# Hedgehog attention beside a Mish layer: the sum of phi(k) times v, two heads crossed in 64 columns or four heads apart in 32

## The chip, the cores and the metric

One core of one Trainium2 chip runs the whole program. The time is the device time of one execution in microseconds (us). The kernel before was run three times: 153.95, 154.15 and 154.91 us, so the median is 154.15 us. A separate execution was recorded by the profiler; the rows shown come from it. Engines are named as in the profile: PE (TensorE matmul; PEld are its weight loads), DVE (VectorE), ACT (ScalarE), POOL (GpSimd), SP (SyncE, which issues most of the transfers).

## The reference: what is computed

```python
def _A_ref(x, wqkv, w_phi, wo):                 # S = 2048, D = 448, H = 16 heads, Dh = 28
    q, k, v = ...                               # x @ wqkv, split into heads
    pq = jnp.einsum("bhsd,hdf->bhsf", q, w_phi)
    pk = jnp.einsum("bhsd,hdf->bhsf", k, w_phi)
    phi_q = jnp.concatenate([_softmax(pq, axis=-1), _softmax(-pq, axis=-1)], axis=-1)
    phi_k = jnp.concatenate([_softmax(pk, axis=-1), _softmax(-pk, axis=-1)], axis=-1)
    kv = jnp.einsum("bhsf,bhsd->bhfd", phi_k, v)
    z  = jnp.einsum("bhsf->bhf", phi_k)
    num = jnp.einsum("bhqf,bhfd->bhqd", phi_q, kv)
    den = jnp.einsum("bhqf,bhf->bhq", phi_q, z)[..., None] + 1e-6
    return (num / den, heads put side by side) @ wo

def _B_ref(x, w1, b1, w2):                      # F = 1792
    h = x @ w1 + b1
    return (h * tanh(softplus(h))) @ w2         # Mish

xn = _layernorm(x)
return x + _A_ref(xn, ...) + _B_ref(xn, ...)
```

The change concerns `kv` and `z`: for each head a sum over all 2048 tokens of phi(k), 28 positive and 28 negative features, times v (28 columns) and times ones.

## The kernel before, in words

The 2048 tokens are 16 tiles (t) of 128, taken in eight pairs (u). Layer norm runs on DVE, ACT and POOL, and the normalized pairs are transposed, by PE at the start and by DMA later. From them PE makes v (`v_mm`), the exponents of k (`k_mm`) and of q (`q_mm`), and the hidden layer of the Mish branch in 28 pieces (`ffn1`, f0.n and f1.n, each in two parts of 8 and 6 matmuls; all these matmuls are issued at line 438). Each takes a pair of PSUM banks out of four pairs; the planner's `take2` gives the pair used least recently, and `free2` gives it back.

ACT writes exp(+-k) into `E_of(u)`. `k_norm` (steps kn u.s) sums it per head on DVE (L631), inverts the sums (L633), and POOL multiplies the product phi(k) in place (L635). ACT also makes the exponentials of q (L684) and Mish (L703); it loads another table between the two.

`v_all` holds, for each token and head, the 28 columns of v and two columns of ones, so that the same matmul gives `kv` and `z`. `kv_mm` (steps kv2 kv3 kv5 kv1 kv4 kv6 kv0 kv7, line 652) adds a pair of tokens tiles to one PSUM bank: the stationary operand is 60 columns of `v_all`, two neighbouring heads, and the moving one the 2 x 56 features of the same two heads. Its results stand in two groups of rows, 0 to 59 and 64 to 123 (r = 0, 1). A result thus holds four blocks: two of a head with itself, and two of one head with the other, which are not wanted. `kvz` (L664, two operations on DVE) adds the epsilon of the denominator (`epsT`, made in `eps_rows`), multiplies by `mask2`, which is 1 on the wanted blocks and 0 on the crossed ones, and writes `KVT` as bf16. Then one DMA transpose (kvT, L670, queue of SP) turns `KVT` into `KVZ`.

The steps nd0 to nd15 (line 726) multiply the transposed phi(q) (`EqT`, DMA transposes at L692, steps e0 to e15) with `KVZ`: for each tile 16 matmuls of 56 rows and 60 moving columns. DVE makes numerator over denominator from the result (L741 to L752). Then come the output projection, the second matmul of the Mish branch (L866, L828, L844), the sum with x on DVE (L793) and the stores.

POOL begins with constants: `mask` (pm), `Wbd` (pw), the zero columns of phi(q) (pp), `mask2` and zeros in `KVT` (pk, L350 to L359), the identity `ident` (pi), later the ones in `v_all` (pv). The identity is used by PE's transposes, the first of which are at L561.

The order of all steps is written out by hand in `ORDER`; each engine does its share of the steps in that order. Waits are put in by the program from what each step reads and writes. Behind the sums the order is: kv7, f1.13 part 1, f1.7 part 1, f0.5 part 1, kvz, f0.8 part 1, and then the second parts; nd3 is the first nd, and e15, e1 and e0 stand behind kvT in SP's queue.

Of the kernel before, what the change touches and what calls it, by code (L numbers as in the profile page):

```python
# [30 lines left out]
def ap_on(src, dims):  # L31
    return bass.AP(tensor=src.tensor, offset=src.offset, ap=[list(src.ap[0])] + [list(d) for d in dims])
# [112 lines left out]


ORDER = """
pm pw lx3s pp pk lx1s lkms lkts st6d lpa table pi st7a st2d st3d rs3t xn3d lvms rs1a z16 xn1d bd wtk0b wtk1b lx2s xt3b
pv xt1d wmk0b wmk1a lqT0 st5a st4d lqT2 rs2a v31a lqT1 lqT3 qd lx6s v11a lx4s v32d wmq1a lx0s k11 xn2p st15d st14d st10d
l1m0s wmq0a st8d rs7p k12 xn7p st1d st9d k31 xt2m q11 l1m1s k32 v12d rs4p st12d xt7m st11d q31 q12 q32 q21 xn4d rs5p  # L150
st13d v21d rs6a q22 xn5d st0d xt4m k21 xt5m v22d v71a k22 v72a rs0p k71 l1m2s k41 kn3.1 e3 k72 k42 xn6d v41a v51a ep e4
k51 xn0p v42a xt6m kn7.0 e2 k52 v52a kn1.1 xt0m kn7.1 kn5.0 v61a lbs q41 v62d kn4.0 k61 q42 e5 e6 l1ts v01d kn2.1 k62
q51 v02d e7 q52 kn1.0 k01 b1 e10 k02 q61 kn3.0 f1.21 e9 q62 e11 f1.22 f1.31 f0.21 e12 e8 f1.51 e13 f1.32 f1.52 kn5.1 los
f0.22 q71 kn2.0 q01 q72 l2s f0.11 f1.01 kn6.1 q02 f1.02 kn6.0 f0.12 kn4.1 kv2 kv3 kv5 kv1 kv4 kn0.0 kn0.1 kv6 kv0 kv7
f1.131 f1.71 f0.51 kvz f0.81 f1.72 f0.52 f0.82 f1.132 f1.81 f0.131 f1.82 nd3 e15 f1.11 e1 e0 f0.132 f1.12 f1.121 nd2
f1.91 f1.122 nd0 f0.101 f1.92 f0.71 f0.102 nd1 f0.72 f1.41 f0.01 ot1m nd6 e14 f1.42 f0.02 f0.91 f0.31 f0.92 ot0m nd7
f0.32 f0.41 wob f1.101 f0.111 f0.42 f0.61 f1.102 f0.112 nd5 f0.62 f1.111 nd4 f0.121 f1.112 f1.61 f0.122 wo01 f1.62 ot3m
ot2m nd11 nd13 G02 wo11 wo32 nd12 G01 nd10 G11 wo22 wo02 ot6m ot5m G31 wo21 nd15 wo31 G21 G32 G12 wo12 sto1 G62 nd14 nd9
G61 wo51 wo61 G51 G22 ot7m G42 sto0 sto3 nd8 ot4m wo52 G41 wo7F g14 wo62 wo7H wo41 G52 stt14 wo42 sto2 g15 sto5 sto4
# [9 lines left out]
def _kernel(es, nc, A_x, A_wqkv, A_w_phi, A_wo, B_w1, B_b1, B_w2, out):  # L169
    def sb(name, shape, dtype):  # L170
        return es.enter_context(nc.sbuf_tensor(name, shape, dtype))
# [5 lines left out]
    mask = sb("mask", [GP, 4], FP32)  # L177
    Wraw = sb("Wraw", [GP, G, DH], BF16)
    Wbd = sb("Wbd", [GP, G, 2, 64], BF16)
    mask2 = sb("mask2", [P, 2, DH], FP32)  # L180
    b1_rows = sb("b1_rows", [FC, P], BF16)
    b1T = sb("b1T", [P, FC], FP32)
    x_all = sb("x_all", [P, NT, D], BF16)
# [43 lines left out]
    def E_of(u):  # L227
        return actT[:, FE + u, 0:4 * D].rearrange("p (s i d) -> p s i d", s=2, i=2)
# [21 lines left out]
    def bank(b, n=1):  # L250
        return PS[:, b * TCW:(b + n) * TCW]
# [89 lines left out]
        op("POOL", lambda e: e.memset(ap_on(v_flat[:, DH:DH + 2].bitcast(mybir.dt.uint32),  # L341
                                            [[(DH + 2) // 2, NU * 2 * H]]), 0x3F80), w=[("v1",)], tag="pv0")

    def p_pads():
        for i in (1, 2, 0):
            op("POOL", lambda e, i=i: e.memset(Eq_of(i).rearrange("p i s (h n) -> p (i s h) n", n=64)[:, :, QP:64], 0.0),
               w=[("Eqp", i)] + ([(n, h) for n in ("WT", "WU") for h in range(2)] if i == 0 else []), tag=f"pp{i}")

    def p_mask2():
        op("POOL", lambda e: e.memset(mask2[:], 1.0), w=[("mask2",)], tag="pk0")  # L350
        for r in range(2):
            lo, hi = HALF[r]
            op("POOL", lambda e, lo=lo, hi=hi: e.affine_select(
                out=mask2[lo:hi], in_=mask2[lo:hi], compare_op=ALU.is_ge, fill=0.0, base=0, channel_multiplier=1,
                pattern=[[-(DH + 2), 2], [0, DH]]), r=[("mask2",)], w=[("mask2",)], tag="pk1")
            op("POOL", lambda e, lo=lo, hi=hi: e.affine_select(
                out=mask2[lo:hi], in_=mask2[lo:hi], compare_op=ALU.is_ge, fill=0.0, base=DH + 1, channel_multiplier=-1,
                pattern=[[DH + 2, 2], [0, DH]]), r=[("mask2",)], w=[("mask2",)], tag="pk2")
        op("POOL", lambda e: e.memset(KVT[:, :, :, :, :].rearrange("p g s x f -> p (g s x f)").bitcast(mybir.dt.uint32),  # L359
                                      0), r=[("mask2",)], w=[("KVT", 0), ("KVT", 1)], tag="pk3")  # L360

    def eps_rows():
        for i in range(2):
            op("DVE", lambda e, i=i: e.tensor_reduce(epsT[:, i:i + 1], ap_on(ident[:, DH + i:DH + i + 1],
                                                                          [[64, 2], [DH + 2, 2]]), AX.XY, ALU.add),
               r=[("ident",)], w=[("epsT", i)], tag=f"ep{i}")
        op("DVE", lambda e: e.scalar_tensor_tensor(epsT[:, 2:3], epsT[:, 0:1], DEN_EPS / 2, epsT[:, 1:2], ALU.mult,
                                                   ALU.add), r=[("epsT", 0), ("epsT", 1)], w=[("epsT", 2)], tag="ep2")
# [149 lines left out]
    def xT(u, eng):  # L518
        i = u % NXN
        if eng == "DMA":  # L520
            dma("SP", lambda e: e.dma_start_transpose(xnT[:, u, :, :], xn[i][:, :]),
                r=[("xn", i, 0, 0), ("xn", i, 1, 0), ("xn", i, 1, 1)] + ([] if u == 1 else [("x", t) for t in (0, NT - 1)]),
                w=[("xnT", u), ("xnU", u)], tag=f"xTm{u}")
            return
        if eng == "both":
            b = take2(False)
            pe(lambda e: transpose7(e, b, xn[i], 3), [("xn", i, 0, 0), ("xn", i, 1, 0), ("xn", i, 1, 1), ("ident",)],
               [pb(b), pb(b + 1)], f"xT{u}")
            evac("ACT", lambda: xnT[:, u, 0:3, :].rearrange("p c n -> p (c n)"), lambda: bank16(b)[:, 0:3 * P], [pb(b)],
                 [("xnT", u)], f"xTe{u}")  # L530
            evac("DVE", lambda: xnT[:, u, 3:7, :].rearrange("p c n -> p (c n)"), lambda: bank16(b + 1)[:, 0:4 * P],
                 [pb(b + 1)], [("xnU", u)], f"xTf{u}")
            return
        b = take1()
        pe(lambda e: transpose7(e, b, xn[i]), [("xn", i, 0, 0), ("xn", i, 1, 0), ("xn", i, 1, 1), ("ident",)], [pb(b)],
           f"xT{u}")
        evac(eng, lambda: xnT[:, u, :, :].rearrange("p c n -> p (c n)"), lambda: bank16(b)[:, 0:7 * P], [pb(b)],
             [("xnT", u), ("xnU", u)], f"xTe{u}")
# [102 lines left out]
    def kv_mm(u):  # L641
        if not kv_seen:
            kv_bank.append(take2())
        kvb = kv_bank[0]
        kv_seen.add(u)
        first, last = len(kv_seen) == 1, len(kv_seen) == NU

        def f(e):
            for par in range(2):
                for g in range(G):  # L650
                    for r in range(2):
                        ins = e.matmul(bank(kvb)[64 * r:64 * r + NDW, g * 2 * QP:(g + 1) * 2 * QP],  # L652
                                       v_all[:, u, par, 8 * r + 2 * g:8 * r + 2 * g + 2, :],
                                       E_of(u)[:, :, par, (4 * r + g) * QP:(4 * r + g + 1) * QP],
                                       start=(first and par == 0 and g == 0), stop=(last and par == 1),
                                       skip_group_check=True)
            return ins
        pe(f, [("E", u, 0), ("E", u, 1), ("v", u), ("v1",)], [pb(kvb)], f"kv{u}")

    def kvz():  # L660
        kvb = kv_bank[0]
        for r in range(2):
            lo, hi = 64 * r, 64 * r + NDW
            op("DVE", lambda e, r=r, lo=lo, hi=hi: e.scalar_tensor_tensor(  # L664
                ap_on(KVT[lo:hi, 0, 0, r, 0:1], [[P, 2 * G], [1, QP]]),
                ap_on(bank(kvb)[lo:hi, 0:1], [[QP, 2 * G], [1, QP]]), epsT[lo:hi, 2:3],
                ap_on(mask2[lo:hi, 0, 0:1], [[0, 2 * G], [1, QP]]), ALU.add, ALU.mult),
               r=[pb(kvb), ("mask2",), ("epsT", 2)], w=[("KVT", r)], tag=f"kvz{r}")
        free2(kvb)
        dma("SP", lambda e: e.dma_start_transpose(KVZ[:, :, :], KVT[:, :, :, :, :].rearrange("p g s x f -> p (g s x f)")),  # L670
            r=[("KVT", 0), ("KVT", 1)], w=[("KVZ",)], tag="kvT")

# [43 lines left out]
    def nd(t):  # L718
        b = take2(False)

        def f(e):
            for s in range(2):
                for g in range(G):
                    for r in range(2):
                        at = (s * G + g) * NDW
                        ins = e.matmul(bank(b + r)[:, at:at + NDW], EqT[64 * r:64 * r + QP, t, s * G + g, :],  # L726
                                       KVZ[64 * r:64 * r + QP, 2 * g + s, 64 * r:64 * r + NDW], start=True, stop=True)
            return ins
        pe(f, [("EqT", t), ("KVZ",)], [pb(b), pb(b + 1)], f"nd{t}")
        i = t % 2  # L730
# [218 lines left out]
    add("b1", bias_T)  # L949
    add("ep", eps_rows)  # L950
    add("qd", double_qT)
    for n, fn in (("pi", p_ident), ("pm", p_mask), ("pw", p_wbd), ("pv", p_ones), ("pk", p_mask2), ("pp", p_pads)):
        add(n, fn)
    for n in (4, 8, 10, 12, 14, 16, 18, 20):
        add(f"z{n}", warm, n)

# [52 lines left out]
```

## Time and profile before

| | |
|---|---|
| median of three runs | 154.15 us (153.95 to 154.91) |
| the profiled execution | 154.01 us |
| its span, first to last instruction | 152.1 us |
| instructions in it | 4002 |
| mean granted clock of PE | 1.000 |
| HBM read and written | 7.02 MB and 1.84 MB |

The profiled execution takes 1.9 us more than its span, for what lies around the first and the last instruction, and it is 0.14 us below the median. A row of the timeline or of the chain begins with the start and the duration in us; a row of a group has the line, the engine, the operation, the result and its sources, the shapes, the count, the busy time in us, the mean of one in ns, and behind the second bar the idle time before it and what ended it. A matmul's own duration covers its way through the array, so many are in flight at once; the pace is read from the time of a run of them.

### The profile page before, as it was taken

Reading aid. Unit: us, or ns where it says so; the run is one execution under the profiler, and the core shown is the slowest. Engines: PE = TensorE matmul, PEld = TensorE weight load, DVE = VectorE, ACT = ScalarE, POOL = GpSimd, SP = SyncE. Lnnn points to the kernel's source line nnn. Section 1 sums busy time; section 2 is a strip of 40 time slices with the busy share of each in tenths; the row PEclk is TensorE's granted clock in tenths of the full one; section 3 lists DMA queues with packets and bytes.
Section 4 is the critical chain, followed back from the end, with each engine's and each line's share of the span. In section 5 each row is a group of like instructions: output and inputs, shape, how many; then the busy total and the mean of one; then the engine's idle time right before and its main releaser. Section 6 shows DMA issues by size and latency. Waiting matters only on the chain.

```text
span 152.1 us, 4002 instructions
## 1 busy us (share of the span) xinstructions
PE 145.4 (96%) x1735; PEld 76.1 (50%) x1735; DVE 102.4 (67%) x224; ACT 74.1 (49%) x96; POOL 41.4 (27%) x59
## 2 busy tenths in 40 slices
PE   7799997999899999999989999999999999999993
PEld 3475543556455584445434445444555555554552
DVE  0997999999999503059998378999373377252452
ACT  3889989796979994776756387100000000000000
POOL 7704743799899970000000000000000000000000
PEclk9999999999999999999999999999999999999999
DMA  5999759989999998840913510803300016003025
GB/s 136 294 136 337 156 166 161 251 158 136 198 190 173 251 271 207 157 89 0 98 37 59 39 26 0 65 2 65 60 0 4 16 49 181 0 4 60 0 100 201
DMA packets 39997, 17.24 MB, mean 113 GB/s; under 512 B 33964, under 2 KB 39212, under 8 KB 39980
## 3 DMA queue, kind: packets, MB, share of 16 engines
q1 hardware_dynamic: 39372, 16.87, 53.5%
q8 instruction: 13, 0.21, 0.6%
q10 hardware_dynamic: 608, 0.12, 0.4%
q14 instruction: 4, 0.03, 0.1%
HBM read 7.02 MB, written 1.84 MB: 58 GB/s over the span
## 4 chain that ended last, share of the span: by engine, by line
PE 69%; DVE 18%; SPq 6%; DMA 3%; ACT 2%; issue 1%
PE PS L438 32%; PE PS L866 28%; DVE stats L467 4%; PE PS L828 3%; SPq L285 3%; DMA x_all<-in_A_x_dram 3%; DVE v_all L745 3%; DVE v_all L747 2%; PE PS L652 2%; PE PS L726 2%; DVE v_all L749 2%; DVE xn L752 2%; DVE v_all L516 1%; DVE mv L468 1%; ACT actT L684 1%
## 5 line engine op out<-in xcount | busy, mean ns | idle before, releaser
L438 PE MATMUL PS<-xnT,W 64*128 64x512 bf16 x392 | 44.9, 376 | 0.9 <-ACT actT L623 0.5
L866 PE MATMUL PS<-W,actT 64*128 64x448 bf16 x392 | 38.7, 349 | 0.0
L703 ACT ACTIVATE actT<-PS,b1T 128x1024 bf16<-128x1024 f32 x28 | 29.8, 1113 | 13.4 <-PE PS L438 13.3
L438 PEld LDWEIGHTS PS<-xnT,W 64*128 64x128 bf16 x392 | 18.9, 94 | 21.7 <-DVE v_all L747 0.9
L866 PEld LDWEIGHTS PS<-W,actT 64*128 64x128 bf16 x392 | 18.8, 94 | 17.2
L635 POOL TENSOR_TENSOR actT<-actT,rSk 128x896 bf16<-128x896 bf16 x16 | 26.6, 1702 | 1.9 <-DVE rSk L633 1.3
L793 DVE TENSOR_TENSOR x_all<-PS,x_all 128x448 bf16<-128x448 f32 (+1 forms) x16 | 9.1, 615 | 15.8 <-PE PS L866 15.1
L631 DVE TENSOR_REDUCE Sk<-actT 128x32 f32<-128x896 bf16 x16 | 16.8, 1047 | 0.2
L741 DVE COPY Sq<-PS 128x16 f32<-128x16 f32 x32 | 4.0, 167 | 17.1 <-PE PS L726 17.0
L623 ACT ACTIVATE actT<-PS 128x896 bf16<-128x896 f32 x16 | 13.7, 923 | 1.0 <-PE PS L438 0.9
L438 PE MATMUL PS<-Wpk,xnT 64*128 64x448 bf16 x112 | 12.9, 350 | 1.0 <-DVE rSk L633 0.8
L438 PE MATMUL PS<-Wkv,xnT 64*128 64x448 bf16 x112 | 12.6, 349 | 0.0
L438 PE MATMUL PS<-Wpq,xnT 64*128 64x448 bf16 x112 | 12.5, 349 | 0.0
L467 DVE BATCH_NORM_STATS2 stats<-x_all 128x6 f32<-128x448 bf16 x14 | 8.5, 607 | 4.3 <-DMA x_all<-in_A_x_dram 4.3
L749 DVE TENSOR_TENSOR v_all<-v_all 128x464 f32<-128x464 f32 x16 | 10.3, 642 | 0.6
L745 DVE TENSOR_TENSOR v_all<-PS,Sq 128x464 f32<-128x464 f32 x16 | 10.3, 641 | 0.5
L752 DVE TENSOR_TENSOR xn<-v_all,rden 128x448 bf16<-128x448 f32 x16 | 10.0, 625 | 0.6
L747 DVE TENSOR_TENSOR v_all<-PS,Sq 128x464 f32<-128x464 f32 x16 | 10.1, 630 | 0.0
L684 ACT ACTIVATE actT<-PS 128x896 bf16<-128x896 f32 x10 | 8.6, 912 | 1.4 <-PE PS L438 1.4
L438 PEld LDWEIGHTS PS<-Wpk,xnT 64*128 64x128 bf16 x112 | 5.5, 94 | 5.8 <-DVE rSk L633 1.2
L438 PEld LDWEIGHTS PS<-Wpq,xnT 64*128 64x128 bf16 x112 | 6.0, 94 | 4.8
L438 PEld LDWEIGHTS PS<-Wkv,xnT 64*128 64x128 bf16 x112 | 5.8, 94 | 4.8 <-issue 0.6
(88 smaller groups left out, 128.8 us busy)
## 6 DMA issues: line engine op xcount, KB each, us to landing
W<-in_B_w_dram SPq DMA_DIRECT2D x1, 1568.0 KB, 7.5
out_dram<-x_all SPq DMA_DIRECT2D x7, 224.0 KB, 2.1
W<-in_B_w_dram SPq DMA_DIRECT2D x3, 448.0 KB, 4.2
x_all<-in_A_x_dram SPq DMA_DIRECT2D x4, 224.0 KB, 3.8
x_all<-in_A_x_dram SPq DMA_DIRECT2D x2, 448.0 KB, 4.2
Wkv<-in_A_wqkv_dram SPq DMA_DIRECT2D x2, 336.0 KB, 4.6
Wo<-in_A_wo_dram SPq DMA_DIRECT2D x2, 336.0 KB, 5.0
W<-in_B_w_dram SPq DMA_DIRECT2D x2, 224.0 KB, 4.8
```

Of the source, the lines that this page charges most:

```text
L438: ins = e.matmul(o, lhs(c, k), rhs(c, k), start=part == "1" and c == 0, stop=part == "2" and c == 2)
L467: op("DVE", lambda e: e.bn_stats(stats[:, t, :], x_all[:, t, :]), r=[("x", t)], w=[("st", t)], tag=f"bn{t}")
L623: op("ACT", lambda e, s=s: e.activation(E_of(u)[:, s, :, :], two(b, D), ACT.Exp, scale=1.0 if s == 0 else -1.0), r=[pb(b), pb(b + 1)], w=[ ...
L631: op("DVE", lambda e: e.tensor_reduce(Sk[u][:, s, :], Eh(), AX.X, ALU.add), r=[("E", u, s)], w=[("Sk", u, s)], tag=f"Sk{u}.{s}")
L635: op("POOL", lambda e: e.tensor_tensor(Eh(), Eh(), ap_on(rSk[u][:, s, 0:1], [[1, 2 * H], [0, DH]]), ALU.mult), r=[("E", u, s), ("rSk", u, ...
L684: op("ACT", lambda e, s=s: e.activation(Eq_of(u)[:, :, s, :].rearrange("p i (h n) -> p i h n", n=64)[:, :, :, 0:QP], two(b, D).rearrange(" ...
L703: op("ACT", lambda e: e.activation(actT[:, fc, q * 1024:(q + 1) * 1024], bank(b, 2), ACT.Mish, bias=b1T[:, fc:fc + 1]), r=[("b1T",), pb(b) ...
L745: op("DVE", lambda e: e.tensor_tensor(tv(t1[i]), num(0), sx(1), ALU.mult), r=[pb(b), pb(b + 1), ("Sq", i, 1)], w=[("t1", i)], tag=f"ta{t}")
L747: op("DVE", lambda e: e.tensor_tensor(tv(t2), num(1), sx(0), ALU.mult), r=[pb(b), pb(b + 1), ("Sq", i, 0)], w=[("t2",)], tag=f"tb{t}")
L749: op("DVE", lambda e: e.tensor_tensor(t1[i], t1[i], t2, ALU.add), r=[("t1", i), ("t2",)], w=[("t1", i)], tag=f"tc{t}")
L752: op("DVE", lambda e: e.tensor_tensor(o_sb[(t // 2) % 2][:, t % 2, :].rearrange("p (h d) -> p h d", d=DH), t1[i][:, :, 0:DH], ap_on(rden[i ...
L866: ins = e.matmul(bank(places[par][0])[:, 0:D], l, r, start=fresh[par], stop=places[par][2] and i >= len(todo) - 2)
```

## The change

`kv_mm` makes the sum for each head apart. Instead of two heads in 60 stationary columns and 112 moving ones there is one head, 30 stationary and 56 moving columns, and four heads stand in four groups of 32 columns of the array; a step has 32 matmuls instead of 16. No crossed blocks arise, so `mask2` and its making on POOL go. `kvz` becomes four additions on DVE, each on 30 rows and on half the columns. The rows of the second head in a group of 64 begin at 32 instead of 30, so `eps_rows` gathers from rows 32 apart, and nd reads `KVZ` as two runs of 30 columns. Zeros in `KVT` now stand for themselves (`KVT0`). The three zero fills `pp` become three steps in the same order; the rest of `ORDER` is the same. A tag is renamed in `xT`.

```diff
-pm pw lx3s pp pk lx1s lkms lkts st6d lpa table pi ...
+pm pw lx3s pp1 pp2 pp0 pk lx1s lkms lkts st6d lpa table pi ...
...
-    mask2 = sb("mask2", [P, 2, DH], FP32)
...
-    def p_mask2():
-        op("POOL", lambda e: e.memset(mask2[:], 1.0), w=[("mask2",)], tag="pk0")
-        for r in range(2):
-            lo, hi = HALF[r]
-            op("POOL", lambda e, lo=lo, hi=hi: e.affine_select(
...
-            op("POOL", lambda e, lo=lo, hi=hi: e.affine_select(
...
+    def p_zero():
         op("POOL", lambda e: e.memset(KVT[:, :, :, :, :].rearrange("p g s x f -> p (g s x f)").bitcast(mybir.dt.uint32),
-                                      0), r=[("mask2",)], w=[("KVT", 0), ("KVT", 1)], tag="pk3")
+                                      0), w=[("KVT0",)], tag="pk3")
...
             op("DVE", lambda e, i=i: e.tensor_reduce(epsT[:, i:i + 1], ap_on(ident[:, DH + i:DH + i + 1],
-                                                                          [[64, 2], [DH + 2, 2]]), AX.XY, ALU.add),
+                                                                          [[32, 4]]), AX.X, ALU.add),
...
             for par in range(2):
                 for g in range(G):
-                    for r in range(2):
-                        ins = e.matmul(bank(kvb)[64 * r:64 * r + NDW, g * 2 * QP:(g + 1) * 2 * QP],
-                                       v_all[:, u, par, 8 * r + 2 * g:8 * r + 2 * g + 2, :],
-                                       E_of(u)[:, :, par, (4 * r + g) * QP:(4 * r + g + 1) * QP],
+                    for j in range(4):
+                        h = 8 * (j // 2) + 2 * g + j % 2
+                        ins = e.matmul(bank(kvb)[32 * j:32 * j + DH + 2, g * QP:(g + 1) * QP],
+                                       v_all[:, u, par, h, :], E_of(u)[:, :, par, h * DH:(h + 1) * DH],
                                        start=(first and par == 0 and g == 0), stop=(last and par == 1),
...
-        for r in range(2):
-            lo, hi = 64 * r, 64 * r + NDW
-            op("DVE", lambda e, r=r, lo=lo, hi=hi: e.scalar_tensor_tensor(
-                ap_on(KVT[lo:hi, 0, 0, r, 0:1], [[P, 2 * G], [1, QP]]),
-                ap_on(bank(kvb)[lo:hi, 0:1], [[QP, 2 * G], [1, QP]]), epsT[lo:hi, 2:3],
-                ap_on(mask2[lo:hi, 0, 0:1], [[0, 2 * G], [1, QP]]), ALU.add, ALU.mult),
-               r=[pb(kvb), ("mask2",), ("epsT", 2)], w=[("KVT", r)], tag=f"kvz{r}")
+        for j in range(4):
+            lo, hi = 32 * j, 32 * j + DH + 2
+            op("DVE", lambda e, j=j, lo=lo, hi=hi: e.tensor_scalar(
+                ap_on(KVT[lo:hi, 0, 0, j // 2, (j % 2) * DH:(j % 2) * DH + 1], [[P, 2 * G], [1, DH]]),
+                ap_on(bank(kvb)[lo:hi, 0:1], [[DH, 2 * G], [1, DH]]), epsT[lo:hi, 2:3], 0.0, op0=ALU.add, op1=ALU.add),
+               r=[pb(kvb), ("KVT0",), ("epsT", 2)], w=[("KVT", j)], tag=f"kvz{j}")
...
-                                       KVZ[64 * r:64 * r + QP, 2 * g + s, 64 * r:64 * r + NDW], start=True, stop=True)
+                                       KVZ[64 * r:64 * r + QP, 2 * g + s, 64 * r:64 * r + 64].rearrange(
+                                           "p (h c) -> p h c", c=32)[:, :, 0:DH + 2], start=True, stop=True)
```

More of the change, by code (lines that the diff above doesn't have):

```diff
@@ L147 @@
 ORDER = """
[L148 to L156, printed above, removed]
+pm pw lx3s pp1 pp2 pp0 pk lx1s lkms lkts st6d lpa table pi st7a st2d st3d rs3t xn3d lvms rs1a z16 xn1d bd wtk0b wtk1b
+lx2s xt3b pv xt1d wmk0b wmk1a lqT0 st5a st4d lqT2 rs2a v31a lqT1 lqT3 qd lx6s v11a lx4s v32d wmq1a lx0s k11 xn2p st15d
+st14d st10d l1m0s wmq0a st8d rs7p k12 xn7p st1d st9d k31 xt2m q11 l1m1s k32 v12d rs4p st12d xt7m st11d q31 q12 q32 q21
+xn4d rs5p st13d v21d rs6a q22 xn5d st0d xt4m k21 xt5m v22d v71a k22 v72a rs0p k71 l1m2s k41 kn3.1 e3 k72 k42 xn6d v41a
+v51a ep e4 k51 xn0p v42a xt6m kn7.0 e2 k52 v52a kn1.1 xt0m kn7.1 kn5.0 v61a lbs q41 v62d kn4.0 k61 q42 e5 e6 l1ts v01d
+kn2.1 k62 q51 v02d e7 q52 kn1.0 k01 b1 e10 k02 q61 kn3.0 f1.21 e9 q62 e11 f1.22 f1.31 f0.21 e12 e8 f1.51 e13 f1.32 f1.52
+kn5.1 los f0.22 q71 kn2.0 q01 q72 l2s f0.11 f1.01 kn6.1 q02 f1.02 kn6.0 f0.12 kn4.1 kv2 kv3 kv5 kv1 kv4 kn0.0 kn0.1 kv6
+kv0 kv7 f1.131 f1.71 f0.51 kvz f0.81 f1.72 f0.52 f0.82 f1.132 f1.81 f0.131 f1.82 nd3 e15 f1.11 e1 e0 f0.132 f1.12 f1.121
+nd2 f1.91 f1.122 nd0 f0.101 f1.92 f0.71 f0.102 nd1 f0.72 f1.41 f0.01 ot1m nd6 e14 f1.42 f0.02 f0.91 f0.31 f0.92 ot0m nd7
 f0.32 f0.41 wob f1.101 f0.111 f0.42 f0.61 f1.102 f0.112 nd5 f0.62 f1.111 nd4 f0.121 f1.112 f1.61 f0.122 wo01 f1.62 ot3m
@@ L342, in p_ones, with p_pads @@
                                             [[(DH + 2) // 2, NU * 2 * H]]), 0x3F80), w=[("v1",)], tag="pv0")
-    def p_pads():
-        for i in (1, 2, 0):
+    def p_pads(which):
+        for i in which:
             op("POOL", lambda e, i=i: e.memset(Eq_of(i).rearrange("p i s (h n) -> p (i s h) n", n=64)[:, :, QP:64], 0.0),
                w=[("Eqp", i)] + ([(n, h) for n in ("WT", "WU") for h in range(2)] if i == 0 else []), tag=f"pp{i}")
-    def p_mask2():
-        op("POOL", lambda e: e.memset(mask2[:], 1.0), w=[("mask2",)], tag="pk0")
-        for r in range(2):
-            lo, hi = HALF[r]
-            op("POOL", lambda e, lo=lo, hi=hi: e.affine_select(
-                out=mask2[lo:hi], in_=mask2[lo:hi], compare_op=ALU.is_ge, fill=0.0, base=0, channel_multiplier=1,
-                pattern=[[-(DH + 2), 2], [0, DH]]), r=[("mask2",)], w=[("mask2",)], tag="pk1")
-            op("POOL", lambda e, lo=lo, hi=hi: e.affine_select(
-                out=mask2[lo:hi], in_=mask2[lo:hi], compare_op=ALU.is_ge, fill=0.0, base=DH + 1, channel_multiplier=-1,
-                pattern=[[DH + 2, 2], [0, DH]]), r=[("mask2",)], w=[("mask2",)], tag="pk2")
+    def p_zero():
         op("POOL", lambda e: e.memset(KVT[:, :, :, :, :].rearrange("p g s x f -> p (g s x f)").bitcast(mybir.dt.uint32),
-                                      0), r=[("mask2",)], w=[("KVT", 0), ("KVT", 1)], tag="pk3")
+                                      0), w=[("KVT0",)], tag="pk3")
     def eps_rows():
@@ L529, in xT @@
             evac("ACT", lambda: xnT[:, u, 0:3, :].rearrange("p c n -> p (c n)"), lambda: bank16(b)[:, 0:3 * P], [pb(b)],
-                 [("xnT", u)], f"xTe{u}")
+                 [("xnT", u)], f"xTh{u}")
             evac("DVE", lambda: xnT[:, u, 3:7, :].rearrange("p c n -> p (c n)"), lambda: bank16(b + 1)[:, 0:4 * P],
@@ L661, in kvz @@
         kvb = kv_bank[0]
-        for r in range(2):
-            lo, hi = 64 * r, 64 * r + NDW
-            op("DVE", lambda e, r=r, lo=lo, hi=hi: e.scalar_tensor_tensor(
-                ap_on(KVT[lo:hi, 0, 0, r, 0:1], [[P, 2 * G], [1, QP]]),
-                ap_on(bank(kvb)[lo:hi, 0:1], [[QP, 2 * G], [1, QP]]), epsT[lo:hi, 2:3],
-                ap_on(mask2[lo:hi, 0, 0:1], [[0, 2 * G], [1, QP]]), ALU.add, ALU.mult),
-               r=[pb(kvb), ("mask2",), ("epsT", 2)], w=[("KVT", r)], tag=f"kvz{r}")
+        for j in range(4):
[4 more added lines that the diff above has]
+               r=[pb(kvb), ("KVT0",), ("epsT", 2)], w=[("KVT", j)], tag=f"kvz{j}")
         free2(kvb)
         dma("SP", lambda e: e.dma_start_transpose(KVZ[:, :, :], KVT[:, :, :, :, :].rearrange("p g s x f -> p (g s x f)")),
-            r=[("KVT", 0), ("KVT", 1)], w=[("KVZ",)], tag="kvT")
+            r=[("KVT", j) for j in range(4)], w=[("KVZ",)], tag="kvT")
     def feat_works(W, cols, q, rows):
@@ L951, in _kernel @@
     add("qd", double_qT)
-    for n, fn in (("pi", p_ident), ("pm", p_mask), ("pw", p_wbd), ("pv", p_ones), ("pk", p_mask2), ("pp", p_pads)):
+    for n, fn in (("pi", p_ident), ("pm", p_mask), ("pw", p_wbd), ("pv", p_ones), ("pk", p_zero)):
         add(n, fn)
+    for i in range(3):
+        add(f"pp{i}", p_pads, (i,))
     for n in (4, 8, 10, 12, 14, 16, 18, 20):
```

## The prediction

> **What bounds the kernel now.** I read the page first, for the engines and the clock, then the chain of work that ended last, then the groups by shape, then the timeline around the changed stage.
>
> ```profile
> PE 145.4 (96%) x1735; PEld 76.1 (50%) x1735; DVE 102.4 (67%) x224; ACT 74.1 (49%) x96; POOL 41.4 (27%) x59
> ...
> PEclk9999999999999999999999999999999999999999
> ...
> q8 instruction: 13, 0.21, 0.6%
> ```
>
> TensorE (PE) is busy for 96% of the span at a full granted clock: what lengthens or shortens its work moves the end, unless another engine stands close behind. The chain shows the stage that the change rewrites, and what follows it:
>
> ```profile
> 54.16 3.27 PE PS L652 x128
> 57.42 8.53 PE PS L438 x78
> 65.95 0.22 PE PS L726 x16
> 66.17 3.02 PE PS L438 x28
> ...
> 122.05 0.44 PE PS L726 x32
> ```
>
> The eight steps kv2 to kv7 are the 128 matmuls of line 652: 3.27 us, or 2.1% of the span, all on the chain. No saving inside this stage can exceed 3.27 us. Line 438 runs 28 matmuls in 3.02 us, 0.108 us each. An nd step (line 726) takes 0.22 us for 16.
>
> ```profile
> L652 PE MATMUL PS<-actT,v_all 128*60 128x112 bf16 x128 | 3.3, 213 | 0.0
> L726 PE MATMUL PS<-KVZ,EqT 56*128 56x60 bf16 x256 | 5.9, 187 | 0.6 <-DVE v_all L747 0.6
> L652 PEld LDWEIGHTS PS<-actT,v_all 128*60 128x60 bf16 x128 | 3.2, 108 | 0.4 <-ACT actT L684 0.4
> 54.40 0.41 PE L652 MATMUL PS<-actT,v_all 128*60 128x112 bf16 x10
> 54.45 0.41 PE L652 MATMUL PS<-actT,v_all 128*60 128x112 bf16 x10
> 54.50 0.21 PEld L652 LDWEIGHTS PS<-actT,v_all 128*60 128x60 bf16 x6
> 54.55 0.21 PEld L652 LDWEIGHTS PS<-actT,v_all 128*60 128x60 bf16 x6
> ```
>
> The first three rows are groups by shape, the last four are the timeline at two instants 50 ns apart. A matmul lives 213 ns, but the oldest of the ten in flight moves on by 0.05 us, which is two matmuls' share (3.27 us / 128 = 25.5 ns each): they run in pairs, one in each 64-column half of the array, one pair per 51 ns, and weight loads move by the same step.
>
> **What stands around that stage.** The timeline:
>
> ```profile
> 52.51 3.36 POOL L635 TENSOR_TENSOR actT<-actT,rSk 128x896 bf16<-128x896 bf16 x2
> 54.09 3.33 PE L652 MATMUL PS<-actT,v_all 128*60 128x112 bf16 x128
> 55.24 1.28 ACT L703 ACT_TABLE_LOAD   x1
> 56.53 2.12 ACT L703 ACTIVATE actT<-PS,b1T 128x1024 bf16<-128x1024 f32 x2
> 57.35 6.00 PE L438 MATMUL PS<-xnT,W 64*128 64x512 bf16 x54
> 57.47 1.38 DVE L664 SCALAR_TENSOR_TENSOR KVT<-PS,epsT,mask 60x448 bf16<-60x448 f32 x2 [5.90 <-PE PS L652]
> 58.87 2.07 SPq L670 DMA_TRANSPOSE KVZ<-KVT  x1
> ...
> KVZ<-KVT SPq DMA_TRANSPOSE x1, 3.3
> ```
>
> Two things here have clock times of their own. POOL finishes the last product phi(k) (steps kn0.0 and kn0.1) at 52.51 + 3.36 = 55.87, and kv0, the seventh of the eight steps, reads it. ACT is kept by its exponentials and a table load until 56.52, and only then empties the two bank pairs of f1.0 and f0.1, at 57.59 and 58.65 (2.12 us for two from 56.53).
>
> **The change part by part.**
>
> *The sum phi(k) v.* 128 pairs of weight load and matmul (60 columns, 112 streamed) become 256 (30 columns, 56 streamed): the streamed columns in all stay 14,336, but over four groups instead of two. Pairs give the price of a group: 51 ns for 112 streamed columns here, and 0.44 us / 16 = 27.5 ns for 60 columns in the x32 row of line 726, where two row halves run side by side. So a column costs about (51 - 27.5) / 52 = 0.45 ns, and four matmuls of 56 columns side by side would take 27.5 - 4 x 0.45 = 25.7 ns. Each step has 32 matmuls, eight such rounds, 0.21 us; eight steps are 1.64 us. That is the lower bound of the stage, 1.63 us below 3.27. The upper bound is that 256 small matmuls keep the spacing of the 128 large ones, 25.5 ns: 6.53 us, 3.26 us more. I take the lower one, because the row nearest in size, line 726, starts a matmul every 13.75 ns and shows no floor above its streaming, and because paired loads of weights stay in step with paired matmuls. [...]
>
> *What the saving meets.* At 0.21 us a step PE comes to kv0 at 54.09 + 6 x 0.21 = 55.35 and waits there for POOL until 55.87. Two steps later, at 55.87 + 0.42 + 0.05 for the release (DVE answers the last kv matmul, 54.16 + 3.27 = 57.43, at 57.47), it is at 56.35 instead of 57.35. Then f1.13, f1.7 and f0.5 open their banks, eight matmuls each, 8 x 0.108 = 0.86 us. Bank pairs go by least recent use: kv holds the first, q0's pair is free for f1.13, f1.7 takes that of f1.0 and f0.5 that of f0.1. f1.13 runs 56.35 to 57.2; f1.7 waits for the first Mish, 57.59, and ends at about 58.5; f0.5 waits for the second, 58.65, and starts at about 58.7. Before, it starts at 57.35 + 2 x 0.86 = 59.07. So about 0.37 us is left of 1.63. If kv0's wait were absent, the two Mish would still leave no more than 0.42. From f0.5 on, PE work is as before, and the banks that it waits for later are given back by work that itself follows PE, so the 0.37 us stays.
>
> *The copy out (kvz).* Two masked operations on 60 x 448 become four unmasked ones on 30 x 224.
>
> ```profile
> L664 DVE SCALAR_TENSOR_TENSOR KVT<-PS,epsT,mask x2: 676/683/690, 57.5 to 58.2; 60x448 bf16<-60x448 f32 x2
> L741 DVE COPY Sq<-PS 128x16 f32<-128x16 f32 x32 | 4.0, 167 | 17.1 <-PE PS L726 17.0
> L745 DVE TENSOR_TENSOR v_all<-PS,Sq 128x464 f32<-128x464 f32 x16 | 10.3, 641 | 0.5
> ```
>
> From 16 elements at 167 ns and 464 at 641, an element costs 1.06 ns; 224 come to 388 ns, four to 1.55 us, against 1.38. The bounds are 4 x 167 = 0.67 and 4 x 683 = 2.73 us. DVE had waited 5.90 us, so nothing else is late on it. The transfer to KVZ starts 0.17 us later behind the sums and lands 3.3 us after: 0.05 + 1.55 + 3.3 = 4.9 us behind the last kv matmul, where the first nd is 8.53 us behind it in the chain. SP's transposes of EqT that stand behind kvT in its queue move by the same 0.17 us. The nearer reader is f0.8, which needs the bank: three openings (2.6 us) after the sums, against 0.1 + 1.55. Cost zero, and at 2.73 us about 0.25.
>
> *POOL's start.* Gone are the memset of mask2 and four selects, and the wait of the KVT memset on them; the three pad steps keep their order.
>
> ```profile
> 2.60 0.14 POOL L350 MEMSET mask<- 128x56 f32 x1
> ...
> 4.00 0.53 POOL L359 MEMSET KVT<- 128x512 uint32 x1
> ...
> 13.21 1.74 POOL L496 TENSOR_SCALAR xn<-x_all,rstd,shift 128x448 bf16<-128x448 bf16 x3 [6.39 <-DVE shift L489]
> ...
> 6.51 1.39 PE L561 MATMUL PS<-ident,Wkv 128*112 128x128 bf16 x16 [0.72 <-DMA Wkv<-in_A_wqkv_dram]
> ```
>
> POOL is 1.40 us earlier with ident, Wbd and the ones. PE's first reader of ident, at 6.51, has waited for the weights by DMA, and POOL's next work waits 6.39 us for DVE. Worth zero; even if its cover went, no more than 0.7 us, PE's wait there.
>
> *The small rest.* epsT sums four elements as before. nd streams KVZ as two runs of 30 instead of one of 60; line 652 already streams two runs of 56 at the price above, so zero, and at one column's price per break 256 / 2 x 0.45 ns = 0.06 us.
>
> *Sum.* The profiled execution took 154.01 us around its span of 152.1. 154.01 - 0.37 = 153.64; the median of the runs, 154.15, stands 0.14 above it, so 153.8 us: a change of -0.2%. A run of this kernel can tell about 1% (1.5 us) from no change.
>
> **The rivals.**
>
> *PE cannot be fed so fast (slower).* The stage would hold 512 instructions of PE. The trace shows 64 in 0.44 us (line 726, 6.9 ns each), but no longer stretch faster than line 652's 256 in 3.27 us, 12.8 ns each; and a queue filled ahead may carry a short burst only. If 12.8 ns is the feed, the stage takes 64 x 6.9 + 448 x 12.8 = 6.2 us, 2.9 more: 157.1. It decides from 9.4 ns an instruction upward (4.8 us, +1.5). For it speaks that no stretch of 512 is seen; against it, that 12.8 ns is fully explained by streaming, so it need not be the feed. [...] Chance 0.24.
>
> *Instructions arrive late by DMA (same or slower).* 3,470 instructions of PE and 13 fetches: one per 267, if q8 is PE's. Each took 0.6% x 16 x 152.1 / 13 = 1.12 us of transport. The stage would need two instead of one. If two follow each other at 1.12 us, POOL's wait covers them; if each is late by as much again, the stage is 4.5 us, +1.2: 155.3. Chance 0.10.
>
> *Weights load one after another (no change).* If the 25.5 ns were two loads of 60 columns taking turns, 256 loads of half the width take the same 3.27 us: 154.15 + 0 to 0.2. Against it stand the loads that move in pairs. Chance 0.20.
>
> *Faster by more than 1%.* Both gates, POOL's at 55.87 and ACT's at 58.65, would have to move with PE, which nothing here makes them do. The whole 1.63 us would then count: 154.15 - 1.63 = 152.5. Chance 0.03.
>
> **How the numbers follow.** The forecast, 153.8, has the remaining 0.43. Forecast, late fetch and turn-taking loads lie between 153.4 (another 0.4 for the last estimates) and 155.5; the range reaches to 157.0, the near half of the feed rival, and leaves out some 0.15. The likeliest one's own range is 153.4 to 154.3. Slower by over 1% are the feed rival (0.24) and a third of the late fetch (0.03): 0.27. Faster 0.03. Within 1% are the forecast, the loads in turn and the rest of the late fetch: 0.43 + 0.20 + 0.07 = 0.70.
>
> **What would show it.** Right: line 652 with 256 matmuls of 30 columns in groups of four starting together, a pause of up to half a microsecond before kv0 with POOL as its releaser, idle time of PE before f1.7 and f0.5 with ACT as releaser, and the first nd some 0.4 us earlier than 65.95. kvz four times near 0.39 us. POOL ready about 1.4 us sooner, and PE's first transposes still at about 6.5. Wrong: a stage of 4.8 us or more with evenly spaced matmuls (feed), a hole inside it without a releaser (fetch), or spacing near 12.8 ns (loads in turn).

## The result, and the profile after

The changed kernel takes 160.3 us (median of four runs, 159.15 to 161.81), the kernel before 154.05 us beside it: a ratio of 1.0375, with a 95% interval of 1.0285 to 1.0465. It is slower by some 6 us. The prediction had 153.8 us, with a range up to 157.0.

The profiled execution took 159.77 us around a span of 157.5. Three lines of the page, to be held against the same three of before:

```profile
PE 147.4 (94%) x1863; PEld 76.2 (48%) x1863; DVE 102.5 (65%) x226; ACT 74.1 (47%) x96; POOL 40.4 (26%) x54
...
PEclk9999999999999995699999999999999999999999
...
q8 instruction: 14, 0.23, 0.7%
```

There are 128 more matmuls and as many more weight loads, two more operations on DVE, five fewer on POOL, and one more fetch of instructions. In two of the 40 slices the granted clock of PE is down to 0.5 and 0.6; before it was full everywhere. The chain of the changed kernel (start, duration, what) tells where the time went:

```profile
56.04 0.45 PE PS L643 x36
56.48 3.29 issue
59.77 0.52 PE PS L643 x26
60.29 11.10 PE PS L428 x63
71.39 0.22 PE PS L715 x16
```

"issue" is time in which the engine waited for nothing that the profile shows. Here it is 3.29 us in the middle of the sums (line 643, before line 652). Behind it, the same run of line 428 up to the first nd takes 11.10 us where it took 8.53, 2.57 us more. The first nd is 71.39 - 65.95 = 5.44 us late, and the whole span is 157.5 - 152.1 = 5.4 us longer. So all of the loss arises between the start of the sums and the first nd. The timeline of PE and DVE there, and the windows (busy time of PE, PEld, DVE, ACT, POOL, then the granted clock, the DMA share, GB/s):

```profile
54.03 1.82 PE L643 MATMUL PS<-actT,v_all 128*30 128x56 bf16 x192
...
56.04 0.45 PE L643 MATMUL PS<-actT,v_all 128*30 128x56 bf16 x36 [0.19 <-POOL actT L625]
...
59.77 0.52 PE L643 MATMUL PS<-actT,v_all 128*30 128x56 bf16 x28 [3.29 <-issue]
60.22 3.59 PE L428 MATMUL PS<-xnT,W 64*128 64x512 bf16 x16
...
56.40:59.70 3.30, 0.08 (x9) 0.00 (x0) 0.00 (x0) 2.18 (x3) 0.24 (x1) 0.84 1.02 334
60.20:65.60 5.40, 5.40 (x34) 1.91 (x28) 1.79 (x4) 0.00 (x0) 0.00 (x0) 0.51 0.53 126
...
L654 DVE TENSOR_SCALAR KVT<-PS,epsT x4: 439/446/458, 60.3 to 61.7; 30x224 bf16<-30x224 f32 x4
```

The sums themselves run fast, if not quite as fast as was hoped: 192 matmuls, three quarters of them, within 1.82 us, where the lower bound of 1.64 us for all would give 1.23. Then comes the short wait for POOL that was forecast. But only 36 matmuls later PE stops, for 3.3 us, while DMA is busy throughout (share 1.02). When it goes on, its clock is 0.51 up to 65.6 us: pairs of matmuls of line 428 start 0.427 us apart there and 0.216 us apart behind it, twice the time. 5.4 us x 0.49 = 2.6 us is just what that run lost.

The starts of the single matmuls, every fourth of line 643, read from the trace of the changed kernel, show the rate in ns, from one round of four to the next:

```
rounds 1 to 8:    38  26  26  25  26  26  26  32
rounds 9 to 47:   31 to 36 each (one of 98)
rounds 49 to 56:  39  25  26  26  26  26  26  32 (behind the wait for POOL)
rounds 58 to 63:  46  46  47  47  46  47 (behind the hole, at the lower clock)
```

Four column groups do run together: 26 ns for four matmuls, where 25.7 was forecast. That holds for eight rounds, 64 instructions. Then it is 33.6 ns on average for the eight instructions of a round, 4.2 ns each. Behind the wait for POOL eight rounds go at 26 ns again, so the slower rate is not the limit of the four groups.

### The profile page after: what moved, and what is told of

Same layout as the page of the kernel before. It is cut to its first block, busy times and chain, and to the rows that moved or that the text cites. A ratio compares the mean times of both kernels' runs of the same rounds, so it can differ in the third digit from the quotient of the medians.

```text
span 157.5 us, 4255 instructions
## 1 busy us (share of the span) xinstructions
PE 147.4 (94%) x1863; PEld 76.2 (48%) x1863; DVE 102.5 (65%) x226; ACT 74.1 (47%) x96; POOL 40.4 (26%) x54
## 4 chain that ended last, share of the span: by engine, by line
PE 58%; DVE 15%; POOL 9%; DMA 5%; SPq 5%; issue 3%; ACT 2%
PE PS L856 27%; PE PS L428 25%; POOL actT L625 9%; PE PS L818 3%; SPq L284 3%; DMA xnT<-xn 3%; DVE stats L457 3%; DVE v_all L735 2%; DMA x_all<-in_A_x_dram 2%; DVE v_all L737 2%; PE PS L715 2%; DVE v_all L739 2%; DVE xn L742 2%; ACT actT L673 1%; DVE mv L458 1%
## 5 line engine op out<-in xcount | busy, mean ns | idle before, releaser
L428 PE MATMUL PS<-xnT,W 64*128 64x512 bf16 x392 | 47.4, 392 | 0.8 <-DVE v_all L737 0.5
L428 PEld LDWEIGHTS PS<-xnT,W 64*128 64x128 bf16 x392 | 19.4, 97 | 23.6 <-issue 3.5
```

Of the source, the lines that this page charges most:

```text
L428: ins = e.matmul(o, lhs(c, k), rhs(c, k), start=part == "1" and c == 0, stop=part == "2" and c == 2)
```

## The experiments

The theory that these rows suggest, called A: PE's instructions come by DMA in pieces of 256 (queue q8 moves 0.23 MB in 14 packets, 16 KB each, for the 3,726 matmuls and weight loads of the changed kernel, and 3,726 / 256 = 14.6; before it was 13 for 3,470, and 3,470 / 256 = 13.6). The next piece is asked for when PE enters the one before it; this is an assumption, as the asking is in no trace. The sums have 512 instructions and run through a whole piece in about 1.1 us, the next has not landed, and PE stands. C is the second part: standing idle lets the clock fall, to 0.51 here. Lines shift from kernel to kernel; the sums are line 643, 652, 654 or 631, and `PS<-actT,v_all` names them in each row.

**Where the hole lies.** The warming matmuls at the start are cut in four, so that 96 more instructions stand ahead of the sums.

```diff
-            for _ in range(n):
-                ins = e.matmul(bank(b)[:, :], ap_on(one, [[0, P]]), ap_on(one, [[0, TCW]]), start=True, stop=True)
+            for _ in range(4 * n):
+                ins = e.matmul(bank(b)[:, 0:P], ap_on(one, [[0, P]]), ap_on(one, [[0, P]]), start=True, stop=True)
```

> The 16 warming matmuls of 512 columns at the very start become 64 of 128 columns: the same work for PE, but 96 more instructions of PE ahead of the sums. Theory A (PE's instructions arrive in pieces of 256, and the stage uses up one piece before the next has landed): the place of the hole moves back by those 96 instructions, from behind the 228th matmul of the sums to about the 180th; its length stays 3 to 4 us, the time stays near 160 us. Theory B (something in the stage itself, a queue that runs dry after so many small matmuls or the form with four column groups, stops PE): the hole stays behind the 228th matmul.

Measured: 161.48 us (before 153.55 beside it; one execution of each). The timeline of PE in this run:

```profile
55.88 1.65 PE L643 MATMUL PS<-actT,v_all 128*30 128x56 bf16 x180
62.25 0.81 PE L643 MATMUL PS<-actT,v_all 128*30 128x56 bf16 x76 [4.73 <-issue]
```

The hole has moved from behind the 228th matmul to behind the 180th: 48 matmuls or 96 instructions, exactly. In these two kernels it sits at a fixed place in the whole stream of PE's instructions, not at a place in the stage. Theory B falls. The length was 4.73 us, above what was expected.

**The number of instructions, without the four groups.** The kernel before, with its two groups and its mask, but each matmul of the sums cut in two by sign.

```diff
-                    for r in range(2):
-                        ins = e.matmul(bank(kvb)[64 * r:64 * r + NDW, g * 2 * QP:(g + 1) * 2 * QP],
...
-                                       E_of(u)[:, :, par, (4 * r + g) * QP:(4 * r + g + 1) * QP],
+                    for s in range(2):
+                        for r in range(2):
+                            at = (2 * g + s) * QP
+                            ins = e.matmul(bank(kvb)[64 * r:64 * r + NDW, at:at + QP],
...
+                                           E_of(u)[:, s, par, (4 * r + g) * QP:(4 * r + g + 1) * QP],
```

> The kernel before, with two heads crossed, the mask and two 64-column groups, but each matmul of the sums is cut in two along its columns (the positive and the negative features): 256 matmuls, 512 instructions as in the changed kernel. Theory A (late instructions): a hole of 2 to 3.4 us inside or right behind the sums, a slower clock of PE after it, 157 to 160 us. Theory B (the four column groups cause the stop): no hole; 256 matmuls of 56 columns in pairs take about 3.4 us and the time is within 154 to 154.6 us.

Measured: 161.22 us in one execution, and the same hole behind the same 228th matmul:

```profile
54.18 3.60 PE L654 MATMUL PS<-actT,v_all 128*60 128x56 bf16 x228
61.34 0.95 PE L654 MATMUL PS<-actT,v_all 128*60 128x56 bf16 x28 [3.56 <-issue]
```

So 256 instructions more do it in the old layout too. Time and hole are a little above what was expected.

**As few instructions as before, with the four groups.** The counterpart: the changed kernel with the second token tile of each pair left out of the sums, and the same cut in the kernel before.

```diff
-            for par in range(2):
+            for par in range(1):
...
-                                       start=(first and par == 0 and g == 0), stop=(last and par == 1),
+                                       start=(first and par == 0 and g == 0), stop=last,
```

> The changed kernel with the same half of the tokens left out of the sums: 128 matmuls of 56 columns in four groups, as many instructions of PE as in the kernel before. Theory A (the loss comes from 256 instructions more, through their fetch): no hole in the sums, full clock, a stage that ends with POOL's gate, 153.3 to 154.0 us. Rival (four groups, the four operations of kvz, the gaps in KVZ or the missing work on POOL cost something by themselves): 155 us or more.

> The kernel before, but the sums leave out the second token tile of each pair (half of the tokens; the output differs by that): 64 matmuls, 256 - 128 instructions, 1.63 us of PE less. Theory G (the gates of the prediction: kv0 waits for POOL until 55.9 us, f1.7 and f0.5 wait for the two Mish of ACT until 57.6 and 58.7 us): of 1.63 us no more than 0.2 to 0.6 us shows, 153.3 to 153.7 us. Rival H (PE is the only bound): all of it shows, 152.2 to 152.5 us.

Measured, in twelve executions of each: four groups 154.26 us, ratio to before 1.0024 (0.9995 to 1.0054); two groups 153.74 us, ratio 0.9987 (0.9961 to 1.0012). No hole is in either; what holds PE up are the two gates of the prediction, in the timeline of the four groups and then of the two:

```profile
56.53 0.39 PE L643 MATMUL PS<-actT,v_all 128*30 128x56 bf16 x32 [0.73 <-POOL actT L625]
...
58.46 2.47 PE L428 MATMUL PS<-xnT,W 64*128 64x512 bf16 x20 [0.57 <-ACT actT L692]
```

```profile
56.19 0.58 PE L652 MATMUL PS<-actT,v_all 128*60 128x112 bf16 x16 [0.53 <-POOL actT L635]
56.71 1.04 PE L438 MATMUL PS<-xnT,W 64*128 64x512 bf16 x8
57.91 2.26 PE L438 MATMUL PS<-xnT,W 64*128 64x512 bf16 x18 [0.16 <-ACT actT L703]
```

Taking 1.63 us of work from PE here changes the time by nothing that can be measured. The gates are real. In these two traces the first nd starts 66.17 - 54.85 = 11.32 and 65.61 - 54.30 = 11.31 us behind the sums, in that of before 65.78 - 54.09 = 11.69 us: 0.37 and 0.38 us less, just what the prediction left of the saving, and too little to show in the times. The medians stand 0.26 us (four groups) and 0.04 us (two) above the ranges given, less than the intervals can tell. Neither the four groups nor kvz, the gaps in KVZ or POOL's missing work cost 1% here; that is shown for half of the sums.

**What makes the piece late.** The load of W2 (1568 KB) goes behind the transposes e1 and e0; in a second kernel the loads of Wo go there too; and the kernel before gets the first move alone.

```diff
-kn5.1 los f0.22 q71 kn2.0 q01 q72 l2s f0.11 ... nd3 e15 f1.11 e1 e0 f0.132
+kn5.1 los f0.22 q71 kn2.0 q01 q72 f0.11 ... nd3 e15 f1.11 e1 e0 l2s f0.132
```

> The changed kernel, but the 1568 KB load of W2, which SP issues at 54.2 us into the middle of the sums, is issued behind the transposes e1 and e0 instead, after the sums. Theory A1 (the fetch of instructions is late because this load fills the DMA engines): the hole shrinks below 1.5 us, the clock of PE stays full, and the time comes to 154 to 156 us. Theory A2 (the fetch has its own latency whatever else moves): the hole stays at 2.5 us or more and the time near 160 us.

> The run with the late load of W2 once more, now timed: theory A gives 155 to 156.5 us, a hole of 2.0 to 2.5 us without a fall of the clock, 1 to 1.6% above before and well below the 3.7% of the changed kernel.

> As the run with the late load of W2, but the four loads of Wo (issued from 49 to 53 us) go behind the sums as well, so that no load from HBM is under way when the sums ask for instructions. Theory A1 (the fetch of instructions waits behind other transfers): with both away the hole is shorter still, under 2.1 us. Rival A2 (what is left, about 3.5 us from asking to use, is the fetch's own): the hole stays at 2.0 to 2.4 us. Time 155 to 156.3 us in both, full clock.

> The kernel before with the load of W2 moved as in the run with the late load, and nothing else. It prices that move by itself. All theories: W2 is used some 30 us after its new place, so the time stays within 0.5% of before; if it is slower by 1% or more, part of what the run with the late load kept over before (2.6 us) belongs to the move and not to the sums.

Measured: W2 late 156.17 us in one execution, and 157.88 us as the median of four others, ratio to before 1.0257 (1.0195 to 1.0319); both late 156.89 us (four), ratio 1.0135 (1.005 to 1.022); the control 153.92 us, ratio 0.9989 (0.9958 to 1.0019). The timelines, W2 late (the single one, then one of the four), then both late:

```profile
54.65 2.05 PE L643 MATMUL PS<-actT,v_all 128*30 128x56 bf16 x228
58.81 0.36 PE L643 MATMUL PS<-actT,v_all 128*30 128x56 bf16 x28 [2.12 <-issue]
```

```profile
54.64 2.05 PE L643 MATMUL PS<-actT,v_all 128*30 128x56 bf16 x228
59.41 0.37 PE L643 MATMUL PS<-actT,v_all 128*30 128x56 bf16 x28 [2.72 <-issue]
```

```profile
53.55 2.21 PE L643 MATMUL PS<-actT,v_all 128*30 128x56 bf16 x228
58.28 0.52 PE L643 MATMUL PS<-actT,v_all 128*30 128x56 bf16 x28 [2.51 <-issue]
...
57.00:59.00 2.00, 0.72 (x30) 0.50 (x32) 0.15 (x1) 1.11 (x2) 0.00 (x0) 0.71 0.00 0
```

Between A1 and A2 the truth is mixed. With W2 away the hole is shorter, 2.1 and 2.7 us for 3.3, and the ratio to before lower (1.0257 for 1.0375, with intervals that overlap a little); but the hole is neither below 1.5 us (A1) nor at its old time (A2). Taking Wo away as well does not shorten the hole further (2.51 us); whether it saves time is not clear, as the intervals of the two kernels overlap. In the last row DMA moves nothing at all (share 0.00, 0 GB/s) while PE still stands. So other transfers do not explain most of the delay here.

By theory A the missing piece is asked for 256 instructions ahead of the hole, at the sums' 200th instruction, 25 rounds or about 0.85 us into the stage. From that instruction to PE's going on it is 59.77 - 54.9 = 4.9 us in the changed kernel, 58.81 - 55.4 = 3.4 and 59.41 - 55.4 = 4.0 with W2 late, and 58.28 - 54.3 = 4.0 with both late. In the run with more warming matmuls, where W2 is under way too, it is the 104th instruction, 0.4 us into the stage, and 62.25 - 56.3 = 6.0 us. The traces also have the packets of queue q8, and they show where this time goes. In the changed kernel the packet starts at 57.10 us, lands at 58.26, and PE goes on at 59.77. It is alike in all six traces with one hole: the changed kernel, more warming matmuls, the matmuls cut by sign, W2 late twice and both late. PE goes on 1.25 to 1.5 us behind the landing, the packet itself takes 0.9 to 1.4 us, and it starts 2.2 to 3.5 us behind the 256th instruction ahead of the hole with W2 under way, but 1.0 to 1.6 us with W2 late. So with W2 under way the packet starts 0.6 to 2.5 us later, and the rest is there without it.

The times of the run of four with W2 late and of both late lie above what was expected: in three of the four executions of each the mean clock was 0.987 to 0.989, so it fell there too, for about half as long as in three of the four executions of the changed kernel (0.978 or 0.979). The fourth of both late, with the full clock, took 154.97 us.

**The clock by itself.** The kernel before with a pause of PE behind the sums, by three and by five additional sums on DVE, and no instruction of PE added.

```diff
+    def pause():
+        kvb = kv_bank[0]
+        for i in range(3):                                    # 5 in the second kernel
+            op("DVE", lambda e, i=i: e.tensor_reduce(Sk[1 + 2 * i][:, 0, :], ...), r=[pb(kvb), ("E", 7, 0)],
+               w=[("pause",), ("Sk", 1 + 2 * i, 0)], tag="pause")
...
-           rows_of("W1") + [...], then)
+           rows_of("W1") + [...] + ([("pause",)] if (q, fc, part) == (1, 13, "1") else []), then)
```

> The kernel before with a pause of PE alone: three more sums on DVE (1.05 us each, results unused) stand behind the last kv matmul, and the first matmul after the stage waits for them, some 3.2 us. No instruction of PE is added. Theory C (the idle time lets PE's clock fall to half, and that costs about 2.6 us more behind the hole): the granted clock is near 0.5 for some 5 us behind the pause and the time is 159 to 160.5 us. Rival (the slow clock in the changed kernel has another cause): full clock, 157.0 to 157.6 us.

> The kernel before with a pause of PE of about 5.3 us behind the sums (five sums on DVE instead of three, results unused), no instruction of PE added. Theory C2 (the clock falls only when PE is idle through one whole period of some 3.4 us, so 3.17 us did not do it): granted clock near 0.5 for 3 us or more behind the pause, time 160 to 162 us. Rival (idle time alone never lowers the clock here): full clock, 159.2 to 159.8 us.

Measured: 157.42 us with three, 162.08 us with five, one execution of each. Timeline and windows of each:

```profile
60.75 2.98 PE L438 MATMUL PS<-xnT,W 64*128 64x512 bf16 x26 [3.17 <-DVE Sk L663]
...
60.75:66.00 5.25, 5.25 (x50) 2.41 (x52) 1.22 (x2) 0.94 (x1) 0.00 (x0) 1.00 0.54 101
```

```profile
62.97 1.04 PE L438 MATMUL PS<-xnT,W 64*128 64x512 bf16 x4 [5.16 <-DVE Sk L663]
...
62.97:66.00 3.03, 3.03 (x16) 1.12 (x18) 1.22 (x2) 0.00 (x0) 0.00 (x0) 0.50 0.20 38
```

The first expectation was missed: 3.17 us of idle left the clock full, and the loss is 157.42 - 153.55 = 3.9 us, 0.7 us above the pause. With 5.16 us the clock fell to 0.50, and 162.08 - 153.87 = 8.2 us is 3.0 us above the pause. So 5.16 us of idle time were enough to lower the clock, without any more instructions.

The length of the stop alone does not decide: 3.17 us did not do it, nor did 2.72 us in the trace of W2 late, but 2.51 us did in that of both late. In the traces the clock changes only at steps of 3.41 us, counted from where it first became full: in the changed kernel it is full from 4.04 us, at half from 58.66 (16 steps later) to 65.48 (two more), and in both late at half from 57.84 to 61.26, one step. The rows below are the step that ends with the fall, of the changed kernel and of both late, and the step of W2 late in which most of its hole lies, behind which the clock stays full:

```profile
55.24:58.65 3.41, 1.05 (x109) 0.84 (x96) 0.00 (x0) 3.34 (x3) 1.07 (x3) 1.00 0.88 252
54.43:57.84 3.41, 1.31 (x140) 1.10 (x127) 0.00 (x0) 3.38 (x4) 0.91 (x2) 1.00 0.02 5
55.19:58.60 3.41, 1.50 (x180) 1.39 (x167) 0.00 (x0) 3.38 (x4) 1.12 (x3) 1.00 0.13 31
```

In the five traces in which the clock fell near the sums, PE was busy for 0.22 to 1.31 us of the step before the fall; of the steps with a hole behind which it stayed full, none had PE busy for less than 1.48 us. So what counts in these traces is how much of a stop lies in one step, and not its length. Theory C2's whole period without work was not needed: in both late the clock fell behind a step with 1.31 us of work. The trace with three sums has no change of the clock, so where its steps lie is not known; a stop of 3.17 us across two steps would fit.

**The sums spread out.** Their eight steps stand among the parts of f1.0, q0 and f0.1 (W2 late as above), in another order, and kvz stands one part earlier.

```diff
-q71 kn2.0 q01 q72 l2s f0.11 f1.01 kn6.1 q02 f1.02 kn6.0 f0.12 kn4.1 kv2 kv3 kv5 kv1 kv4 kn0.0 kn0.1 kv6 kv0 kv7 f1.131 f1.71 f0.51 kvz
+q71 kn2.0 q01 q72 kv7 kv3 f1.01 kv5 kn6.1 q02 kv1 kv2 f1.02 kn6.0 f0.11 kn4.1 kv6 kv4 f0.12 kn0.0 kn0.1 kv0 f1.131 f1.71 kvz f0.51
```

> The changed kernel with the load of W2 behind the sums, and the eight steps of the sums no longer in one block: they stand among the parts of f1.0, q0 and f0.1, whose 34 matmuls make the stretch some 5.8 us long. 256 instructions then last some 2.6 us instead of 0.9. Theory A (a piece of 256 instructions must not be used up before the next lands, about 3.5 us with the W2 load away): what is left of the hole is at most 1 us at a time, the clock stays full, the gates of ACT cover part of it, and the time is 153.4 to 154.8 us, no more than 0.5% from before. Rival (each piece costs a fixed stop of 2 us and more once the sums are in 256 matmuls, spread or not): 155.5 us or more.

Measured in twelve executions: 153.54 to 156.22 us, median 155.24 against 153.87 before, 0.9% more. Without the three slowest (155.88 to 156.22 us) the ratio is 1.0042 (1.0003 to 1.008). The timeline of PE in one of these three:

```profile
54.63 0.48 PE L631 MATMUL PS<-actT,v_all 128*30 128x56 bf16 x40 [1.06 <-issue]
...
58.63 0.37 PE L631 MATMUL PS<-actT,v_all 128*30 128x56 bf16 x28 [0.40 <-issue]
```

Two holes of 1.06 and 0.40 us are left of one of 3.3, and the clock stays full in all twelve. They stand exactly 256 instructions of PE apart, and PE goes on 1.3 and 1.5 us behind the landing of their packets, as above. The same 256 matmuls cost 0.4 to 0.9% instead of 3.7% when the instructions are used up more slowly. The median of all twelve lies 0.4 us above the range that theory A gave and below the rival's 155.5. It is still no gain over before: the gates leave little to win, and the two holes are 1.5 us together.

## Why the prediction was wrong

The step that failed is the rival "Instructions arrive late by DMA", with its chance of 0.10 and its price of 1.2 us; in the sum of the forecast itself late instructions have no term. The mechanism was named, and so was the number of instructions for each fetch. Its price was taken from the transport of a piece, 1.12 us, doubled. What counted is the time from the 256th instruction ahead of the hole, where theory A puts the asking, to PE's going on: 4.9 us in the changed kernel and 3.4 to 6.0 in the four others above. A row that shows only how long packets move says nothing on how long the asker waits. These 256 instructions last 1.6 us here, 0.4 us of it the wait for POOL, and this leaves a hole of 3.3 us, where the rival had a loss of 1.2.

The second failure is a term that stood nowhere: behind the stop of 3.29 us PE went on at half its clock (0.51). In the changed kernel this cost 2.6 us, nearly as much as the hole's net cost (stage from 54.03 to 60.22, 6.19 us, against 3.26 before: 2.9 us). Together they make the 5.4 us, to 0.1 us.

The other steps, one by one:

- The rate of four groups: 25.7 ns for four matmuls forecast, 26 measured for the first 64 instructions, then 33.6. The lower bound of 1.64 us for the stage was a little low: 8 x 26 + 56 x 33.6 ns = 2.1 us without a hole. Loads of weights taking turns are ruled out: 256 at 12.8 ns would need 51 ns for four.
- "PE cannot be fed so fast": there is a slower rate behind the first 64 instructions, but it is 4.2 ns an instruction, not 12.8, far below the 9.4 from which it would have decided. It had the larger chance of the two slower rivals, and it was the wrong one.
- The gates: POOL ended the wait at 56.04, forecast 55.87 and a little. ACT's gate is hidden by the hole in the changed kernel and shows in both halved kernels. That 1.63 us of PE's work is worth almost nothing here was right, and not by luck: both gates were found, with the 0.37 us that they leave. That the forecast of 153.8 us would have held without the hole is argued, not shown, as no run has the whole sums in four groups without a hole.
- kvz: four times 0.446 us, forecast 0.388; 0.45 us longer than before in all (1.83 for 1.38) and, as said, without cost that shows: KVZ lands at 64.9 us (62.20 and 2.7 to landing), ahead of the first nd.
- POOL's start: the identity is ready at 3.60 + 0.29 = 3.89 us, 1.4 us earlier as forecast, and PE's first transposes still wait for DMA:

```profile
3.60 0.29 POOL L323 TENSOR_SCALAR_AFFINE_SELECT ident<-ident 128x128 bf16<-128x128 bf16 x1
...
6.65 0.62 PE L551 MATMUL PS<-ident,Wkv 128*112 128x128 bf16 x8 [0.61 <-DMA Wkv<-in_A_wqkv_dram]
```

- The signs named for a late fetch, "a hole inside it without a releaser", were the ones that appeared.

## What to carry to other kernels

Count instructions as well as columns: where matmuls are cut smaller at the same number of columns, check how long 256 instructions of PE last, and compare that with the 3.4 to 6.0 us that these runs showed from the 256th instruction ahead of a hole to PE's going on; if it is much less, try to spread them among longer work (here 0.4 to 0.9% over before instead of 3.7%). Before work is taken from the busiest engine, ask which other engine's clock time stands right behind it: here 1.63 us less of PE was worth nothing measurable. And price a stop of PE with what may follow it, not with its length alone: in the changed kernel a time at half the clock, 2.6 us.

## What the runs showed of the hardware that was not expected

- The holes lie on a grid of 256 instructions of PE: 96 instructions more at the start moved the hole by exactly 96, and the two holes of the spread sums are 256 apart. The packets of q8 have 16 KB each, 14 for 3,726 matmuls and weight loads in the changed kernel, and at every hole PE went on only behind the landing of one. With the sums in one run of 256 matmuls the stop was 2.1 to 4.7 us.
- The landing of the packet is not the end of the wait: PE went on 1.25 to 1.5 us behind it in all eight holes.
- In the trace of the changed kernel the first 64 instructions of the sums, and 64 again behind the wait for POOL, go at 26 ns for eight; between them it is 33.6 ns for eight, 4.2 ns each.
- The clock fell to 0.5 with PE idle for 2.51 us, and stayed full through 2.72 and 3.17 us. In the traces it changes at steps of 3.41 us, and the fall came behind steps in which PE had been busy for 1.31 us or less. With 5.16 us of idle it fell too.
